# Filler matmuls in the first batch's TensorE gaps, and a filter copy moved ahead of the evacuations

## Chip, cores, metric

One core of a Trainium2 chip (trn2), nothing else running on it. The metric is the device time of one execution in microseconds (us), lowest is best. "Before" and "after" are the kernel before and after the change. PE is TensorE, DVE VectorE, ACT ScalarE, POOL GpSimd. SBUF is the on-chip memory; to evacuate a matmul's result is to copy it from the matmul's output memory into SBUF. A filler is a matmul whose result nobody uses. The clock of PE that a trace calls granted is 1 at full speed and 0.5 at half (in the kernel before, 0.50 stands beside matmuls of 512 columns that start 0.427 us apart, 1.00 in the main stage beside 0.216); fillers are meant to have it released from half to full.

## The reference

A frequency filter along the sequence, then a two-layer MLP with a leaky ReLU, on the same 24064 x 256 tokens:

```python
x: (8, 3008, 256)                      # batch, seq, dim
X = rfft(x, axis=1); Y = X * (filt_r + 1j * filt_i)[None]
y = irfft(Y, n=3008, axis=1).reshape(24064, 256)
h = y @ w_in                           # 256 -> 2048
out = maximum(0.01 * h, h) @ w_out     # 2048 -> 256
```

## The kernel before

The FFT of length 3008 = 94 x 32 is made of matmuls with constants: stage 1 (contraction over the 94 rows, constant `f1`), a transpose on DVE, stage 2 (`fwd2`), the filter product, stage A of the inverse (`inv2`, `inv2x`), another transpose, stage B (constant `i1`). For batches 1 to 7 this is threaded between the MLP's matmuls. For batch 0 there is nothing to thread it into, so it runs by itself at the start; that is the part that the change touches. Line numbers are those of the kernel before.

```python
R1 = 96; N1 = 94                 # f1 has 96 rows, the last two are zero
f1_sb = cpool.tile([R1, N2, P], FP16)          # loaded first, in four slices
x_load(0, ...)                   # x of batch 0: 96 rows, four slices
...
def first_s1(n0, n, kind, copy):               # stage 1, line 250
    ps = bank(kind, n, D)
    for j in range(n):
        nc.tensor.matmul(ps[:, j, :], f1_sb[:N1, n0 + j, :], x_sb[:N1, n0 + j, :],
                         start=True, stop=True)
    spread(big[0], n0, ps, copy)
def first_s2(hf, c, n, on_pool):               # stage 2, line 259, and the filter product
    src = paired(big[1])                       # pairs of fp16, 128 bytes apart
    for j in range(0, n, 4):
        nc.tensor.matmul(ps[...], fwd2, src[:, ds(c + j, 4), ts(hf, DH // 2)], ...)
    # on_pool: ACT copies (line 267), POOL multiplies (270); else DVE multiplies (275)
def first_sa(hf, c):                           # stage A: line 283, ACT evacuates (284)
...
def upper(hf):                                 # line 307: copy the filter to partitions 64-127
    for t, cp in ((fa_sb, act), (fb_sb, dve)):
        cp(t[64:P, :, ts(hf, DH)], t[0:64, :, ts(hf, DH)])
def keep_warm(n):                              # line 312: results unused
    for _ in range(n):
        nc.tensor.matmul(po_ps..., small_sb[:, 0, :], i1_sb[...][:, 0:512], start=True, stop=True)

for g in range(6):  first_s1(4 * g, 4, "ph", (dve, act)[g % 2])
for g in range(4):  first_s1(24 + 2 * g, 2, ...)
t1_part(0, 0), t1_part(0, 1)                   # DVE transposes, line 193
upper(0)
first_s2(0, 8, 8, True); x_load(1); first_s2(0, 0, 8, False)
...                                            # (cut; the order is in the diff below)
keep_warm(5)
for g in range(16): first_sb(g, ...)           # stage B: line 300, copies 303 (two loops, shortened)
...                                            # main loop: MLP, lines 364, 369, 378, 385
```

## Time and profile before

| | before |
|---|---|
| time, first three runs | 788.86, 789.22, 786.11 us |
| span of the profiled run | 787.1 us |
| first slice of x usable (first line 250) | 9.03 us |
| first transposes (line 193) | 18.21 us |
| first line 259 | 20.73 us |
| first line 300 | 41.35 us |
| first MLP matmul (line 364) | 46.75 us |
| end | 740 us after the last row |

Read it as a prologue of 47 us in which a chain passes from engine to engine, and a main part in which PE is full (busy for 725.27 of the 729 us from 58 us on). The stretches, PE timeline and ACT timeline that carry this are shown in the prediction. Three more lines, from the table of fine stretches of the kernel before (stretch, its length, PE busy and count, granted clock, DMA share, GB/s), mark where the clock falls to half and comes back:

```profile
37.00:37.25 0.25, 0.25 (x2) 0.91 0.03 0
37.25:37.50 0.25, 0.25 (x2) 0.50 0.01 0
...
40.50:40.75 0.25, 0.25 (x2) 0.77 1.32 176
```

The first has 0.91 = 0.5 + 0.5 x 0.82, so the fall is 82% into it, at 37.20; in the last, 54% of the stretch is at full clock, so the return is at 40.62.

Two lines of DVE, which is the chain between PE's stages:

```profile
18.21 2.37 DVE L193 STREAM_TRANSPOSE big<-big 128x1024 f32<-128x1024 f32 x2
22.71 1.23 DVE L275 TENSOR_TENSOR fy_h_c<-ph,fa_sb 128x1024 f16<-128x1024 f32 x1 [1.14 <-ACT fx_h_c L267]
```

### The profile page before, as it was taken

The page shows a single profiled execution, that of the slowest core. Times are in us where ns is not written, and L with a number is a line of the kernel's source. Part 1 is how long each engine was busy: PE and PEld are TensorE (multiplying, and loading weights), DVE is VectorE, ACT ScalarE, POOL GpSimd, SP SyncE. Part 2 cuts the span into 40 slices and gives each one's busy share as a digit, 9 for nine tenths or more (in the row PEclk, how much of TensorE's full clock was granted, in tenths as well). Part 3 has the DMA queues.
Part 4 walks back from the last instruction along what each step waited for, and adds up shares of the span by engine and source line. Part 5 has one row for each costly group of instructions (what it writes and reads, how often), then busy time and mean ns, then how long its engine had stood idle before and what let it go on. Part 6 is the DMA issues. An engine that isn't in the chain of part 4 may idle for free.

```text
span 787.1 us, 13542 instructions
## 1 busy us (share of the span) xinstructions
PE 764.4 (97%) x5777; PEld 526.2 (67%) x5777; DVE 366.2 (47%) x457; ACT 556.1 (71%) x790; POOL 148.8 (19%) x122
## 2 busy tenths in 40 slices
PE   3799999999999999999999999999999999999998
PEld 2256677666776667866777667776677666676666
DVE  3858760784317652386415764078432765200000
ACT  3687768776687767877687775967668776666664
POOL 4772400240003400043000510024000340000000
PEclk9999999999999999999999999999999999999999
DMA  9944010501023010511014101050100101101111
GB/s 177 203 62 99 27 41 28 122 28 41 27 67 83 27 41 27 108 41 42 28 41 107 41 28 42 27 119 28 41 28 27 41 27 41 41 28 41 41 41 55
DMA packets 36252, 43.38 MB, mean 55 GB/s; under 512 B 8130, under 2 KB 34370, under 8 KB 35522
## 3 DMA queue, kind: packets, MB, share of 16 engines
q0 software_dynamic: 10000, 16.99, 12.3%
q1 hardware_dynamic: 26192, 25.53, 9.2%
q8 instruction: 45, 0.74, 0.4%
q14 instruction: 15, 0.12, 0.0%
HBM read 34.10 MB, written 24.64 MB: 75 GB/s over the span
## 4 chain that ended last, share of the span: by engine, by line
PE 94%; ACT 2%; DVE 1%; DMA 1%; issue 1%; POOL 0%; ACTq 0%; DVEq 0%; POOLq 0%
PE po_ps L378 41%; PE ph L364 40%; PE pf L170 3%; PE pf L237 2%; PE pf L225 2%; PE pf L210 2%; DMA x_sb<-in_x_dram 1%; PE pf L378 1%; ACT big L181 1%; DVE fy_h_c L275 1%; PE pf L283 1%; ACT gt_c L369 1%; PE ph L250 0%; ACT fa_sb L307 0%; DVE big L193 0%
## 5 line engine op out<-in xcount | busy, mean ns | idle before, releaser
L369 ACT ACTIVATE gt_c<-ph 128x1024 f16<-128x1024 f32 x376 | 384.8, 1024 | 194.8 <-PE ph L364 193.8
L364 PE MATMUL ph<-yt,w_in_sb 128*128 128x512 f16 (+7 forms) x1728 | 386.6, 351 | 0.4 <-ACT yt L303 0.2
L378 PE MATMUL po_ps<-w_out_sb,gt_c 128*128 128x256 f16 x2944 | 381.5, 272 | 0.6 <-ACT ost_c_t L385 0.6
L378 PEld LDWEIGHTS <-gt_c 128*128 128x128 f16 x3008 | 290.7, 98 | 86.7 <-issue 1.7
L364 PEld LDWEIGHTS <-w_in_sb 128*128 128x128 f16 x1728 | 163.0, 98 | 95.2 <-issue 1.0
L218 POOL TENSOR_TENSOR y_b_g<-p_b_g,p_b_g 128x512 f16<-128x512 f32 x84 | 106.9, 1273 | 225.5 <-DVE p_b_g L216 225.5
L193 DVE STREAM_TRANSPOSE big<-big 128x1024 f32<-128x1024 f32 x32 | 55.9, 1847 | 127.0 <-ACT big L181 126.7
L181 ACT CAST big<-pf 128x512 f16<-128x512 f32 x190 | 109.0, 607 | 0.0
L240 DVE CAST yt<-pf 128x376 f16<-128x376 f32 x112 | 56.3, 545 | 85.9 <-PE pf L237 85.9
L214 DVE TENSOR_TENSOR p_b_g<-pf,fa_sb 128x512 f32<-128x512 f32 x84 | 58.1, 692 | 38.5 <-PE pf L210 35.9
L385 ACT COPY ost_c_t<-po_ps 128x256 f32<-128x256 f32 x184 | 69.4, 377 | 6.7 <-PE po_ps L378 5.6
L201 DVE STREAM_TRANSPOSE big<-big 128x1024 f32<-128x1024 f32 x28 | 51.1, 1935 | 34.5 <-ACT big L181 34.5
L215 DVE TENSOR_TENSOR p_b_g<-pf,fb_sb 64x512 f32<-64x512 f32 x84 | 58.2, 693 | 1.1
L216 DVE TENSOR_TENSOR p_b_g<-pf,fb_sb 64x512 f32<-64x512 f32 x84 | 57.4, 684 | 1.1
L132 POOL DMA_DIRECT2D x_sb<-in_x_dram x12 | 6.6, 553 | 256.6 <-PE pf L170 255.8
L237 PEld LDWEIGHTS <-big 128*128 128x128 f16 x448 | 25.7, 98 | 13.2
L170 PE MATMUL pf<-x_sb,f_sb 94*128 94x256 f16 x224 | 33.8, 272 | 0.1
L210 PE MATMUL pf<-big,small_sb 128*128 128x512 f16 x84 | 31.8, 379 | 0.0
L225 PE MATMUL pf<-y_b_g,small_sb 128*128 128x512 f16 x84 | 31.8, 379 | 0.0
L237 PE MATMUL pf<-i_sb,big 128*128 128x94 f16 x448 | 28.7, 206 | 0.0
L170 PEld LDWEIGHTS <-f_sb 94*128 94x128 f16 x224 | 20.9, 97 | 9.5 <-issue 1.3
L250 PE MATMUL ph<-x_sb,f_sb 94*128 94x256 f16 x26 | 6.2, 412 | 10.1 <-DMA x_sb<-in_x_dram 9.6
(45 smaller groups left out, 154.1 us busy)
## 6 DMA issues: line engine op xcount, KB each, us to landing
out_dram<-ost_c_t SPq DMA_DIRECT2D x92, 256.0 KB, 2.1
x_sb<-in_x_dram POOLq DMA_DIRECT2D x6, 1536.0 KB, 11.0
x_sb<-in_x_dram POOLq DMA_DIRECT2D x4, 384.0 KB, 10.2
w_in_sb<-in_moe_w_in_dram POOLq DMA_DIRECT2D x1, 1024.0 KB, 13.0
w_out_sb<-in_moe_w_out_dram POOLq DMA_DIRECT2D x1, 1024.0 KB, 9.8
x_sb<-in_x_dram POOLq DMA_DIRECT2D x1, 1024.0 KB, 8.0
f_sb<-fwd_const SPq DMA_DIRECT2D x4, 192.0 KB, 5.7
fa_sb<-in_filt_r_dram POOLq DMA_DIRECT2D x4, 192.0 KB, 12.3
```

The lines of the kernel that those rows point to most:

```text
L170: nc.tensor.matmul(ps[:, j, :], f1_sb[:N1, n2, :], x_sb[:N1, n2, :], start=True, stop=True)
L181: copy(paired(dst)[:, ds(n0, nn), ds(e0, de)], ps.rearrange("p n (e t) -> p n e t", t=2))
L214: nc.vector.tensor_tensor(p1[:], ps, fa, AL.mult)
L215: nc.vector.tensor_tensor(p2[0:64], ps[64:P], fb[64:P], AL.mult)
L216: nc.vector.tensor_tensor(p2[64:P], ps[0:64], fb[0:64], AL.mult)
L218: nc.gpsimd.tensor_tensor(y1[:], p1[:], p2[:], AL.add)
L237: nc.tensor.matmul(ps[:, j, :], src[:, dt, n2, :], i1_sb[:, n2, :], start=True, stop=True)
L240: copy(yv[:, :, ds(4 * h, 4)], ps.rearrange("p c a -> p a c"))
L364: nc.tensor.matmul(ph[:, j, ds(o, ln)], w_in_sb[:, dt, ts(ct, P)], yts[b % 2][:, dt, ds(lo, ln)], start=(dt == 0), stop=(dt == NDT - 1),)
L369: nc.scalar.activation(gts[ci][:, ds(2 * g, 2), :], ph, AF.Lrelu)
L378: nc.tensor.matmul(po, gts[ci][:, ct, ts(tj, P)], w_out_sb[:, ct, :], start=(ct == 0), stop=(ct == NCT - 1))
L385: nc.scalar.copy(ost[:, tj % 2, :], po)
```

## The change

Intent: keep PE busy in the prologue so that its clock goes to full early and stays there, and let ACT make the second filter copy while it would wait for PE anyway. 53 fillers are added; all fillers read the forward constant `f1`, which lands first, instead of `small` and `i1`.

```diff
     def keep_warm(n):
         for _ in range(n):
-            nc.tensor.matmul(po_ps.rearrange("p a d -> p (a d)"), small_sb[:, 0, :],
-                             i1_sb[:].rearrange("p a d -> p (a d)")[:, 0:512],
-                             start=True, stop=True)
+            nc.tensor.matmul(po_ps.rearrange("p a d -> p (a d)"), f1_sb[:, 0, :],
+                             f1_sb[:, 0:4, :].rearrange("p a d -> p (a d)"), start=True, stop=True)
+    keep_warm(8)
     for g in range(6):
         first_s1(4 * g, 4, "ph", (dve, act)[g % 2])
+        if g % 2:
+            keep_warm(4)
     for g in range(4):
         first_s1(24 + 2 * g, 2, two[g == 3], (act, dve)[g % 2])
+    keep_warm(12)
     t1_part(0, 0, True)(), t1_part(0, 1, True)()
     upper(0)
     first_s2(0, 8, 8, True)
     x_load(1)
     first_s2(0, 0, 8, False)
     t1_part(0, 2, True)()
+    keep_warm(3)
     first_s2(0, 20, 4, True)
+    keep_warm(4)
     first_s2(0, 16, 4, False)
     t1_part(0, 3, True)()
+    upper(1)
     first_sa(0, 0), first_sa(0, 16)
-    upper(1)
+    keep_warm(3)
     first_s2(1, 8, 8, True)
     first_sa(0, 8), first_sa(0, 20)
     first_s2(1, 0, 8, False)
+    keep_warm(3)
     ...
     first_s2(1, 16, 8, False)
+    keep_warm(4)
     first_sa(1, 0)
+    keep_warm(4)
     first_t2(0), first_t2(1)
```

## The prediction

> **What bounds the kernel now.** I read the page first. TensorE (PE) is busy 97% of a 787.1 us span and 94% of the chain that ended last is PE. The busy times by stretch say where the other 3% is:
>
> ```profile
> span 787.1 us, 13542 instructions
> PE 764.4 (97%) x5777; PEld 526.2 (67%) x5777; DVE 366.2 (47%) x457; ACT 556.1 (71%) x790; POOL 148.8 (19%) x122
> ...
> 0.00:47.00 47.00, 28.56 (x202) 13.72 (x203) 28.49 (x29) 25.51 (x38) 31.24 (x31) 0.96 1.08 181
> 47.00:58.00 11.00, 10.62 (x61) 5.79 (x60) 5.75 (x10) 9.93 (x15) 7.46 (x2) 1.00 0.01 2
> 58.00:787.00 729.00, 725.27 (x5516) 506.71 (x5514) 331.95 (x420) 520.68 (x738) 110.09 (x90) 1.00 0.17 48
> ```
>
> The columns after the length are busy PE, weight loads, DVE, ACT, POOL. From 58 us on PE has 3.7 us of gaps in 729: a prologue that ends earlier passes its gain to the end one for one, and nothing after it changes. The change touches only the 47 us of the first batch (the first matmul of line 364 starts at 46.75), where no engine is full. So the question is when that matmul starts afterwards.
>
> The PE timeline of the prologue carries the argument:
>
> ```profile
> 9.03 1.86 PE L250 MATMUL ph<-x_sb,f_sb 94*128 94x256 f16 x8 [9.03 <-DMA x_sb<-in_x_dram]
> 11.46 1.86 PE L250 MATMUL ph<-x_sb,f_sb 94*128 94x256 f16 x8 [0.57 <-DMA x_sb<-in_x_dram]
> 13.79 1.86 PE L250 MATMUL ph<-x_sb,f_sb 94*128 94x256 f16 x8 [0.46 <-DVE big L181]
> 15.51 1.44 PE L250 MATMUL pf<-x_sb,f_sb 94*128 94x256 f16 x6
> ...
> 20.73 1.88 PE L259 MATMUL ph<-big,small_sb 128*128 128x512 f16 x4 [3.36 <-DVE big L193]
> ...
> 25.53 2.74 PE L283 MATMUL pf<-fy_h_c,small_sb 128*128 128x512 f16 x6
> 28.60 1.03 PE L259 MATMUL ph<-big,small_sb 128*128 128x512 f16 x2 [0.33 <-DVE big L193]
> 29.45 1.91 PE L283 MATMUL pf<-fy_h_c,small_sb 128*128 128x512 f16 x6
> 31.20 1.02 PE L259 MATMUL ph<-big,small_sb 128*128 128x512 f16 x2
> ...
> 36.98 2.96 PE L283 MATMUL pf<-fy_h_c,small_sb 128*128 128x512 f16 x7 [0.74 <-DVE fy_h_c L275]
> 39.73 1.69 PE L312 MATMUL po_ps<-i_sb,small_sb 128*128 128x512 f16 x5
> ```
>
> Starts are 0.427 us apart at 512 columns at 25.53 and again at 36.98 (the last of the seven starts at 39.31), where the main stage has 0.216. That is half clock. In fine stretches the granted clock goes to 0.5 at 37.20 and back to 1 at 40.62, and the spacing of line 283 falls to 0.216 at 30.39. The record prints 1.00 from the start although line 250 runs at 0.213 per 256 columns, so I trust spacings there and not the record. So: half clock to 30.39, full to 37.20, half to 40.62.[...]
>
> **One group does not follow the clock.** The line list of line 259 says 588/607/620 ns (min, median, max) for its 12 matmuls, the same at 31.20, when the clock was full, as at 20.73. Line 283 has a minimum of 376. So warming PE buys nothing in line 259.
>
> [...]A window with some 85% of busy stream (26.97 to 30.38) released it here; one as busy with 94-row matmuls (13.31 to 16.73) did not.[...] Line 259 reads 4-byte pairs 128 bytes apart[...].[...]
>
> **The change part by part.**
>
> Filler: 53 new 128x512 matmuls (8 + 3x4 + 12 + 3 + 4 + 3 + 3 + 4 + 4) beside the 5 old ones (keep-warm, line 312), all on the forward constant with 96 rows. At 0.216 us they cost 11.4 us of PE, at half clock 22.6; PE idles over 18 us here. They write the bank that the main stage uses first near 59 us, so they wait for nobody, but a real matmul behind them waits for them.
>
> Stage 1, to the first transposes (18.21 us before). The x slices land at about 9.03, 11.46, 13.7 and 15.5, and no filler moves that. Filler of 8 runs 3.30 to 6.7, cold. Then 8 real to 10.74, 4 fillers cold to 12.45: the second slice waits 1.0 us for them. PE is now without gaps, so it is released[...]. From there: groups 2, 3 end 13.73; filler to 14.6; group 4 waits for DVE's copy of group 2 (13.5 + 1.23), so 14.8 to 15.2; DVE copies it to 16.6; fillers to 16.5; groups 6 to 9 to 17.36; DVE copies groups 7 and 9 (0.69 each) to 18.5. Transposes at 18.55: **0.35 us later**. A release by 10.7 would give 0.6 earlier; at 15.8 it would be 1.5 later. [...]I take 0.4 later. The 12 fillers then end near 20.0, before the transposes (21.0).
>
> From the transposes to 28.5: transposes 2.37, line 259 x4 at its fixed 0.427, DVE products, transpose, products, transpose. DVE is the chain, unchanged. **0**.
>
> 28.54 to 31.8: line 259 x2 (0.85), line 283 x6 at 0.216 (1.3; before four were cold), line 259 x2 (0.85 + 0.17 drain): DVE's products of the second half start at 31.8 instead of 32.31. **0.5 us gained**.
>
> The moved copy: ACT does its 2.75 us filter copy before the evacuations instead of behind them:
>
> ```profile
> 26.60 0.60 ACT L284 CAST big<-pf 128x512 f16<-128x512 f32 x1 [2.47 <-PE pf L283]
> 27.46 0.61 ACT L284 CAST big<-pf 128x512 f16<-128x512 f32 x1 [0.25 <-PE pf L283]
> 28.31 0.60 ACT L284 CAST big<-pf 128x512 f16<-128x512 f32 x1 [0.24 <-PE pf L283]
> 28.94 2.75 ACT L307 COPY fa_sb<-fa_sb 64x3072 f16<-64x3072 f16 x1
> 31.71 1.07 ACT L267 COPY fx_h_c<-ph 128x512 f32<-128x512 f32 x2
> ```
>
> ACT idled 2.47 us up to 26.60, from 24.14. The copy goes there (24.3 to 27.1; the filter's last part lands near 22 to 23 by its issue at 11.61 and 10.4 us to landing), the three evacuations follow to 28.9, and the copies for POOL come at 29.65 instead of 31.71. So POOL's four products end near 34.9 instead of 36.88. This alone moves no end, because DVE's chain ends at 36.93 too; it keeps POOL from becoming the bound when DVE gets earlier. The DVE half of the move changes no DVE order. DVE then ends its four products at 36.45.
>
> 36.45 to the inverse stage: before, 7 matmuls at 0.427 from 36.98, then fillers (two of five warm) to 41.35. After, warm: 7 x 0.216 to 38.0, fillers to 39.15. ACT's four evacuations at 0.54 each from 36.9 end at 39.1 (before 40.58). Line 300 starts at 39.15 to 39.3 instead of 41.35: **2.1 us gained** in all, of which 0.5 is counted above. Its second half needs the last two transposes, at 39.2 + 2.37 = 41.55, when PE gets there at 41.6: just in time. The inverse stage is bound by ACT's copies and keeps its 5.4 us.
>
> Sum: 2.1 gained at line 300, less 0.4 from stage 1: **1.7 us**, so the first line 364 near 45.0. Loads for the main stage are early: the next batch lands before 39 and is used at 46. 788.86 - 1.7 = 787.1 us.
>
> **Rivals.** (1) The filler in stage 1 does not release the clock: 94- and 96-row work may count less, for which the window at 13.31 speaks. Then 20 cold fillers in the in-order PE stream cost 1.71 us per four and 5.1 for the twelve; transposes come 3.8 us late and line 259 later still: a loss of 3 to 4 us, about 792. Against it: [...]the stream is gapless, not 85%. I give it 12%. (2) The clock is released by the first 8 fillers[...] or a little earlier: stage 1 gains 0.6, total 786.1. 20%. (3) Nothing in effect: DVE and DMA set the pace, PE's clock was never on the path. For it: line 259 is deaf to the clock and DVE is the chain from 18 to 37; against it: seven cold matmuls and a cold filler stand openly between 36.98 and 40.6 with ACT waiting 0.24 before each evacuation. It would leave 788.9. 15%.
>
> **Range and chances.** The three runs before spread from 786.1 to 789.2, as much as the effect. Range 784.7 to 789.4. The whole prologue's PE waits cannot give 2% (15.8 us), nor can the fillers cost it, so within 2% is nearly sure.
>
> **What would show it.** Right: line 250 about 0.107 apart per 256 columns after some 13 us; line 259 still near 0.43; line 283 at 0.216 to the end with no half clock after 30; ACT's second filter copy at about 24.5; line 300 starting between 39 and 40.2; first line 364 between 44.5 and 45.5; nothing changed after. Wrong: line 250 cold to the end with transposes after 20 us, or line 283's last seven still cold, or a start of line 364 within 0.5 us of 46.75.

## The result, and the profile after

After: 790.99 us median (790.50 to 791.14, four runs). Before, with one more run: 788.39 (786.11 to 789.22). The ratio is 1.0036, 95% interval 1.0014 to 1.0059. A ratio here is the mean time of one kernel's fast runs over that of the other's of the same rounds, so not quite the ratio of the medians. All runs are fast: none is over 1.5% above the fastest of its kernel. A gain of 1.7 us was predicted; the change costs some 2.6 us by the medians. The call "within 2%" held; the direction and the range did not.

The PE timeline of the kernel after (start, length, engine, line, operation, shapes, count, idle before it):

```profile
3.25 3.59 PE L312 MATMUL po_ps<-f_sb 96*128 96x512 f16 x8 [3.25 <-DMA f_sb<-fwd_const]
7.97 1.86 PE L250 MATMUL ph<-x_sb,f_sb 94*128 94x256 f16 x8 [1.12 <-DMA x_sb<-in_x_dram]
9.63 1.91 PE L312 MATMUL po_ps<-f_sb 96*128 96x512 f16 x4
11.34 1.91 PE L250 MATMUL ph<-x_sb,f_sb 94*128 94x256 f16 x8
...
18.16 1.48 PE L250 MATMUL pf<-x_sb,f_sb 94*128 94x256 f16 x6
19.45 0.63 PE L250 MATMUL ph<-x_sb,f_sb 94*128 94x256 f16 x2
19.87 5.33 PE L312 MATMUL po_ps<-f_sb 96*128 96x512 f16 x12
24.99 1.91 PE L259 MATMUL ph<-big,small_sb 128*128 128x512 f16 x4
26.72 0.83 PE L312 MATMUL po_ps<-f_sb 96*128 96x512 f16 x3
...
33.72 1.47 PE L283 MATMUL pf<-fy_h_c,small_sb 128*128 128x512 f16 x6
...
40.81 1.68 PE L283 MATMUL pf<-fy_h_c,small_sb 128*128 128x512 f16 x7 [0.37 <-DVE fy_h_c L275]
...
48.91 1.29 PE L373 MATMUL ph<-yt,w_in_sb 128*128 128x512 f16 x4 [0.16 <-ACT yt L303]
```

(Line 373 is line 364 of the kernel before, the MLP.) The stream has no gap from 7.97 to 28.8, and yet each eight of line 250 still take some 1.7 us (1.66 to 1.71) from their start to that of what follows, which is 0.213 per 256 columns: half clock, though the trace prints a granted clock of 1.00 there. Twelve fillers take 5.33. Only the three fillers at 26.72 are quick (0.83 = 2 x 0.216 and a modelled end of some 0.39). So the clock was released between 25.0 and 26.7 (the first clock event in the packed trace is at 25.22), and held from there: line 283 has a median of 378 ns in all its 24 matmuls, where it had 613 before. Line 259's matmuls last 589/607/616 ns (min, median, max), as before (588/607/620).

The DVE timeline of the kernel after shows what this did to the chain:

```profile
19.26 0.69 DVE L181 CAST big<-pf 128x512 f16<-128x512 f32 x1 [2.19 <-PE pf L250]
20.11 0.69 DVE L181 CAST big<-ph 128x512 f16<-128x512 f32 x1 [0.16 <-PE ph L250]
20.92 2.37 DVE L193 STREAM_TRANSPOSE big<-big 128x1024 f32<-128x1024 f32 x2
23.32 0.95 DVE L307 COPY fb_sb<-fb_sb 64x3072 f16<-64x3072 f16 x1
26.99 1.22 DVE L275 TENSOR_TENSOR fy_h_c<-ph,fa_sb 128x1024 f16<-128x1024 f32 x1 [2.72 <-ACT fx_h_c L267]
```

DVE waits 2.19 us for PE before three of its five stage-1 copies, the transposes start at 20.92 instead of 18.21 and end at 23.29, and behind its filter copy DVE idles 2.72 us (1.14 before), since the twelve fillers keep PE from line 259 until 24.99.

**The first slice of x lands at a different time in each run** (7.3 to 9.0 us over the traces here), and all of the prologue moves with it. So I compare intervals from the first line 250 of the same trace. The last stretch, from the first MLP matmul to the measured time, is the same 742.2 to 742.5 us in all traces of these kernels (789.03 - 46.75 before, 791.07 - 48.91 after), so the interval to the first MLP matmul is the whole effect.

| trace | to transposes | to line 259 | line 259 to MLP | in all |
|---|---|---|---|---|
| before, profiled run (slow kind, see below) | 9.18 | 11.70 | 26.02 | 37.72 |
| after | 12.95 | 17.02 | 23.92 | 40.94 |

Up to line 259 the change loses 5.3 us, behind it gains 2.1.

### The profile page after: what moved, and what is told of

Read it like the earlier page. It is cut to its first block, busy times and chain, and to the rows that moved or that the text cites. A ratio compares the mean times of both kernels' runs of the same rounds, so it can differ in the third digit from the quotient of the medians.

```text
span 789.2 us, 13649 instructions
## 1 busy us (share of the span) xinstructions
PE 778.6 (99%) x5830; PEld 532.5 (67%) x5830; DVE 366.1 (46%) x457; ACT 555.7 (70%) x790; POOL 149.0 (19%) x122
## 4 chain that ended last, share of the span: by engine, by line
PE 92%; ACT 2%; DVE 1%; issue 1%; ACTq 0%
PE po_ps L387 40%; PE ph L373 40%; PE pf L170 3%; PE pf L237 2%; PE pf L225 2%; PE pf L210 2%; PE pf L387 1%; ACT big L181 1%; ACT gt_c L378 1%; DVE fy_h_c L275 1%; ACT yt L303 0%; PE ph L300 0%; PE pf L283 0%; ACT ost_c_t L394 0%; DVE big L193 0%
## 5 line engine op out<-in xcount | busy, mean ns | idle before, releaser
L312 PE MATMUL po_ps<-f_sb 96*128 96x512 f16 x58 | 21.5, 519 | 3.3 <-DMA f_sb<-fwd_const 3.3
```

## Experiments

Twelve runs were made, two of them of the kernel before itself, in three groups, each beside eleven runs of the kernel before on the group's chip. Correct results in all. Times are medians.

| run | time | ratio to before (95%) | first line 250 to MLP |
|---|---|---|---|
| late_fill | 786.04 | 0.9986 (0.9967 to 1.0004) | 35.86 |
| ones128 | 786.64 | 0.9987 (0.9970 to 1.0004) | 35.34 |
| ones96 | 791.00 | 1.0048 (1.0031 to 1.0064) | 40.94 |
| fill_only | 791.68 | 1.0058 (1.0044 to 1.0073) | 40.81 |
| move_only | 788.05 | 1.0009 (0.9992 to 1.0026) | 37.78 |
| late128 | 787.01 | 0.9996 (0.9980 to 1.0013) | 35.62 |
| rows96 | 786.97 | 0.9996 (0.9981 to 1.0011) | 35.72 |
| no_twelve | 790.80 | 1.0044 (1.0027 to 1.0060) | 39.61 |
| before_again / before_third | 788.74 / 785.48 | one run each | 37.86 / 35.70 |
| probe_rows / probe_two | 899.17 / 1018.63 | one run each, with bursts behind the end | not used |

Theory after the result: a clock that never was released in stage 1 made the fillers cost PE time on the chain. What had to be found is why a gapless stream did not release it: the number of rows (94 and 96 of 128), the data (the constant has zero columns), or the width.

### late_fill: the fillers of stage 1 taken out

```diff
-    keep_warm(8)
-        if g % 2:
-            keep_warm(4)
-    keep_warm(12)
```

> The changed kernel without the fillers of stage 1 (the first 8, the 3 times 4, the 12): only the later fillers and the moved copy stay. Theory: these 32 fillers cost 4.3 us on the path at half clock and release nothing, while all behind them gains 2.1 us. So transposes at 18.2, line 300 near 39.3, first MoE matmul near 44.7, and 2.1 us under the kernel before: ratio to before 0.9973. Rival (the late part gains only because the long early stream released the clock at 25 to 26.7 us): the clock stays at half past 30 us and the gain is under 1 us.

```profile
17.16 2.37 DVE L193 STREAM_TRANSPOSE big<-big 128x1024 f32<-128x1024 f32 x2
19.68 1.88 PE L259 MATMUL ph<-big,small_sb 128*128 128x512 f16 x4 [3.36 <-ACT fa_sb L307]
```

Measured: transposes at 17.16 (9.23 after the first line 250, as before), line 259 at 19.68, MLP at 43.79. The 32 fillers of stage 1 are what costs. The remainder takes 24.11 us from line 259 to the MLP, 1.9 less than the profiled run of before. But the ratio is 0.9986, not 0.9973: half the expected gain, and its interval holds 1. Neither theory said that; before_again and before_third explain it.

### ones128 and ones96: the same fillers on another tile, 128 or 96 rows

The edit, shortened:

```diff
+    warm_sb = cpool.tile([P, 512], FP16, name="warm_sb")
+    nc.vector.memset(warm_sb[:], 1.0)
-            nc.tensor.matmul(po_ps..., f1_sb[:, 0, :], f1_sb[:, 0:4, :]..., start=True, stop=True)
+            nc.tensor.matmul(po_ps..., warm_sb[:128, 0:P], warm_sb[:128, :], start=True, stop=True)  # ones96: [:96]
```

> The changed kernel with its fillers on a 128-row tile of ones (set by DVE at about 1 us) instead of the 96-row forward constant; same number and places. Theory rows: with half of the stream at 128 rows the clock is released in stage 1, by 9 to 15 us; transposes near 18.0 to 19, line 300 near 39 to 40, ratio to before 0.996 to 0.999. Rival data: ones count less than real values and the clock stays at half to 25 us, ratio 1.003 as after the change.

> As the 128-row kernel of ones, but only 96 rows of the tile are used. Theory rows: cold through stage 1 like the changed kernel, transposes near 20.9, ratio to before 1.003. Rival data (zeros in the forward constant are the cause, not rows): released in stage 1 like 128 rows, ratio under 1.

PE timeline of ones128, then of ones96 (line numbers are two higher here: 252 is stage 1, 314 the filler):

```profile
12.71 1.03 PE L314 MATMUL po_ps<-warm_sb 128*128 128x512 f16 x4
13.57 1.04 PE L252 MATMUL ph<-x_sb,f_sb 94*128 94x256 f16 x8
...
16.19 2.75 PE L314 MATMUL po_ps<-warm_sb 128*128 128x512 f16 x12
```

```profile
12.42 1.91 PE L314 MATMUL po_ps<-warm_sb 96*128 96x512 f16 x4
14.13 1.92 PE L252 MATMUL ph<-x_sb,f_sb 94*128 94x256 f16 x8
...
19.25 5.33 PE L314 MATMUL po_ps<-warm_sb 96*128 96x512 f16 x12
```

Same number of instructions, same values, same places; with 128 rows four fillers take 1.03 us, with 96 rows 1.91. The two differ by 4.8 us in their mean time (786.49 and 791.27). So rows made the difference here and the constant's zeros did not: ones96 behaves like the kernel after (40.94 us from the first line 250 to the MLP in both). In ones128 the path was less simple than expected: its first eight fillers, from 1.46 us, released the clock at 5.73, it fell back at 9.14, after PE had waited 3.37 us for x (up to 8.43), and was released again at 12.56 (times of the clock events in its trace). That fall, and not one near 37 us, is what the 0.998 of its profiled run counts. As an explanation of ones96, "96 rows are too few" was the obvious reading. The next probe says it is not quite that.

### probe_rows and probe_two: bursts of one kind of matmul, each from half clock

Behind the end of the kernel before, bursts whose operands POOL rewrites before each (condensed from probe_two; probe_rows has one pass of POOL and 48 matmuls of 512 columns per burst):

```diff
+    for rows, cols, width in (...):
+        for _ in range(3):
+            nc.gpsimd.tensor_scalar(flat[:, 0:3072], wflat[:, 0:3072], 1.0, 0.0, AL.mult, AL.add)
+        for _ in range(28 * 512 // width):
+            nc.tensor.matmul(po[:cols, :width], flat[:rows, 0:cols], flat[:rows, ds(128, width)], ...)
```

> The kernel before with eight bursts of 48 gapless 128x512 matmuls put behind its end. Before each burst GpSimd rewrites the operands (some 8 us or more, in which TensorE is idle and falls back to half clock). Bursts in order: 128 rows of random weights, 96 rows, 112 rows, 128 rows of zeros, 128 rows of ones, 104 rows, 128 rows with 64 stationary columns, 120 rows. Theory rows ([...]94 to 96 of 128 are too few): 128 rows go from 0.427 to 0.216 us spacing[...]; 96 rows stay at 0.427 for all 48 (20.5 us); somewhere between 96 and 128 lies the limit. Rival data (the structural zeros of the forward constant are what counts too little): 96 random rows release like 128; zeros stay at half clock. Rival busy time alone: all eight release[...], and the cold stretch after the change has another cause.

In probe_rows the idle time was only 2.97 us, too short for this purpose: four of the seven bursts that had a gap before them ran at a granted clock of 0.50 at first, the other three at 1.00 throughout. 96 random rows, 112, 120 and 128 rows with 64 columns were released in these, the first within 6.1 us; zeros, ones and 104 rows never were cold, so they said nothing. The released 96 rows contradict my "96 rows stay at half clock". probe_two makes POOL's pass three times, for a longer idle time (8.64 us).

> Bursts behind the kernel before, as in the first probe, but with three GpSimd passes (some 8 us idle) before each, so that every burst starts at half clock. Each is 12 us long at half clock. In order: 128 rows x 512 columns; 96 x 512; 94 x 512; 94 x 256; 96 x 256; 128 x 256; 88 x 512; 64 x 512; 128 rows with 32 stationary columns x 512; 128 x 512 zeros; 128 x 512 ones; 94 x 256 with the forward constant as weights; 4 times (8 of 94 x 256, 4 of 96 x 512), the mix of stage 1. The first probe has shown 96 random rows released[...], so 96 rows alone are enough. Theory rows[...]: 96 x 512 released[...], 94 x 512 and 88 and 64 not at all, the mix not. Theory width (256-column matmuls count less[...]): 94 x 512 released; 94, 96 and perhaps 128 x 256 and the mix not. Theory weights (the constant's zero columns count less): only the burst with the forward constant as weights is not released. Zeros and ones tell whether data counts at all.

PE timeline of probe_two; a burst that stays at half clock takes 12.1 us, one that starts there and is released some 8:

```profile
796.85 8.08 PE L434 MATMUL po_ps<-x_sb 96*128 96x512 f16 x28 [8.64 <-POOL x_sb L439]
813.57 12.13 PE L434 MATMUL po_ps<-x_sb 94*128 94x512 f16 x28 [8.64 <-POOL x_sb L439]
834.34 12.13 PE L434 MATMUL po_ps<-x_sb 94*128 94x256 f16 x56 [8.64 <-POOL x_sb L439]
855.11 8.01 PE L434 MATMUL po_ps<-x_sb 96*128 96x256 f16 x56 [8.64 <-POOL x_sb L439]
871.77 8.21 PE L434 MATMUL po_ps<-x_sb 128*128 128x256 f16 x56 [8.64 <-POOL x_sb L439]
888.62 12.12 PE L434 MATMUL po_ps<-x_sb 88*128 88x512 f16 x28 [8.64 <-POOL x_sb L439]
909.39 12.13 PE L434 MATMUL po_ps<-x_sb 64*128 64x512 f16 x28 [8.64 <-POOL x_sb L439]
930.16 7.99 PE L434 MATMUL po_ps<-x_sb 128*32 128x512 f16 x28 [8.64 <-POOL x_sb L439]
946.78 8.20 PE L434 MATMUL po_ps<-x_sb 128*128 128x512 f16 x28 [8.64 <-POOL x_sb L439]
963.63 8.31 PE L434 MATMUL po_ps<-x_sb 128*128 128x512 f16 x28 [8.64 <-POOL x_sb L439]
980.58 12.11 PE L434 MATMUL po_ps<-x_sb,f_sb 94*128 94x256 f16 x56 [8.64 <-POOL x_sb L439]
1001.33 13.84 PE L434 MATMUL po_ps<-x_sb 94*128 94x256 f16 x48 [8.64 <-POOL x_sb L439]
```

(The bursts at 946.78 and 963.63 are zeros and ones. The last line is the mix, whose two kinds are merged; 13.84 us is all half clock: 32 x 0.213 + 16 x 0.427 + an end of some 0.17. The first burst, 128 rows, followed the main loop without a gap and was never cold.)

The bursts of 96 rows were released (8.08 us at 512 columns, 8.01 at 256), those of 94 rows were not within their 12.13 us at either width, nor those of 88 and 64 rows (12.12 and 12.13). With 128 rows all were released: 256 columns (8.21), 32 stationary columns (7.99), zeros (8.20) and ones (8.31). So in these bursts neither width nor stationary columns nor data decided it, and **the outcome changes between 94 and 96 rows.** The mix of 94 and 96 rows, that of the kernel after, stays at half clock for its 13.84 us, while ones128's mix of 94 and 128 rows was released, at 12.56.

### rows96: the changed kernel with 96 rows in stage 1

Rows 94 and 95 of the constant are zero, and those of x are in SBUF, so they can be multiplied too:

```diff
-            nc.tensor.matmul(ps[:, j, :], f1_sb[:N1, n0 + j, :], x_sb[:N1, n0 + j, :],
+            nc.tensor.matmul(ps[:, j, :], f1_sb[:R1, n0 + j, :], x_sb[:R1, n0 + j, :],
```

> The changed kernel with one edit: the stage-1 matmuls of line 250 take 96 rows instead of 94 (rows 94 and 95 of the constant are zero and those of x are loaded, so the result is the same). The second probe put the limit between 94 and 96 rows. Theory rows: the same gapless stream now counts as enough, the clock is released near 12 to 16 us, line 250 goes from 0.213 to 0.107 us per 256 columns, transposes near 18.5 instead of 20.9, the twelve fillers end before them, line 300 starts some 21 us after the transposes, and the time is 786 to 787.3, ratio to before 0.996 to 1.000, some 4 us under the changed kernel. Rival (something else in stage 1 holds the clock down): no change, ratio 1.003 or more.

PE timeline of rows96:

```profile
8.93 1.87 PE L250 MATMUL ph<-x_sb,f_sb 96*128 96x256 f16 x8 [1.84 <-DMA x_sb<-in_x_dram]
10.59 1.91 PE L312 MATMUL po_ps<-f_sb 96*128 96x512 f16 x4
12.29 1.30 PE L250 MATMUL ph<-x_sb,f_sb 96*128 96x256 f16 x8
13.43 1.03 PE L312 MATMUL po_ps<-f_sb 96*128 96x512 f16 x4
...
17.08 2.75 PE L312 MATMUL po_ps<-f_sb 96*128 96x512 f16 x12
20.76 1.88 PE L259 MATMUL ph<-big,small_sb 128*128 128x512 f16 x4 [0.93 <-DVE big L193]
```

The clock goes to full inside the second eight of line 250 (1.30 us for the eight where 1.86 is cold), near 12.9. The transposes start at 18.24. Two more rows, and the changed kernel loses 4 us of its time (786.87 mean, where the kernel after has 790.90, and ones96 and fill_only 791.3 and 791.6, in other groups; no_twelve, still with 94 rows, has 790.65 in the same group). This settles the cause of the loss. And it is the working that I had predicted, nearly to the digit: transposes expected at 18.55, line 300 at 39.15 to 39.3 (39.25), first MLP near 45.0 (44.65). But it is no faster than before.

### before_again and before_third: why the gain behind stage 1 is worth so little

> The kernel before, to catch the trace of one of its quick runs (clock printed as 1.0, some 786 us), which are about six in ten. Theory: its quick and slow runs differ in whether the clock falls back near 37 us; in a quick one line 283's last seven matmuls are 0.216 apart and line 300 starts near 39.5 to 40 us after the same load time, some 2 us earlier than in the slow one. Rival: they differ in when the first slice of x lands (7.3 to 9.0 us) and not in the clock.

> The same once more, in case the first falls in the other kind.

PE timeline of before_again (788.74 us), then of before_third (785.48 us):

```profile
8.49 1.86 PE L250 MATMUL ph<-x_sb,f_sb 94*128 94x256 f16 x8 [8.49 <-DMA x_sb<-in_x_dram]
...
36.58 3.15 PE L283 MATMUL pf<-fy_h_c,small_sb 128*128 128x512 f16 x7 [0.74 <-DVE fy_h_c L275]
...
46.35 1.28 PE L364 MATMUL ph<-yt,w_in_sb 128*128 128x512 f16 x4 [0.16 <-ACT yt L303]
```

```profile
7.48 1.87 PE L250 MATMUL ph<-x_sb,f_sb 94*128 94x256 f16 x8 [7.48 <-DMA x_sb<-in_x_dram]
...
35.09 1.67 PE L283 MATMUL pf<-fy_h_c,small_sb 128*128 128x512 f16 x7 [0.73 <-DVE fy_h_c L275]
...
43.18 1.28 PE L364 MATMUL ph<-yt,w_in_sb 128*128 128x512 f16 x4 [0.17 <-ACT yt L303]
```

The kernel before has two kinds of run. In one the clock falls to half near 37 us and the last seven matmuls of line 283 take 3.15 us; in the other they take 1.67, and from line 250 to the MLP it is 35.70 us instead of 37.86. The rest of the 3.3 us between the two times is the landing of x (1.0). The kinds can be told by the mean clock: the 3.42 us at half of the profiled run (37.20 to 40.62) in some 787 us make 1 - 0.0022 = 0.998. Of the 33 runs of before beside the experiments, 21 have 0.999 or 1.0 and a mean of 786.43 us (785.45 to 787.32), 12 have under 0.999 and a mean of 788.83 (787.49 to 789.50). (Two of these have 0.996, for which one fall is not enough; no trace of such a run was kept.) The run that was profiled for the prediction was of the slow kind, and so the "2.1 us" were already there in the quick kind. What decides which kind a run becomes is not shown: PE's last waits before the seven matmuls are 0.83, 0.44, 0.33 and 0.74 us in before_again, where the clock fell, and 1.04, 0.22, 0.33 and 0.73 in before_third, where it did not, so nearly the same in sum (2.34 and 2.32).

### fill_only and move_only: the two parts apart

Move_only is the kernel before with `upper(1)` moved; fill_only is after with it moved back.

> All fillers of the change, but the filter copy left behind the evacuations. Theory: the move has no part in the loss; the fillers alone make it. Time within 0.5 us of the changed kernel, ratio to before 1.003 to 1.005. Rival (the move costs, since the evacuations wait for a 2.75 us copy): under 1.002.

> The kernel before with the filter copy moved and no filler. Theory: DVE's chain ends where it did and POOL's earlier end is unused, so within 0.5 us of before, ratio 0.9995 to 1.0005. Rival (the move costs by itself): 1.002 or more.

Fill_only behaves like the kernel after (40.81 against 40.94 us to the MLP), move_only like before (37.78 in a slow-kind trace, against 37.72 and 37.86). Both ratios missed what was expected: 1.0058 where 1.003 to 1.005 was, 1.0009 where 0.9995 to 1.0005 was. Five of move_only's six runs were of the slow kind, which explains its mean; whether the move makes that kind more frequent is not shown. Fill_only's profiled run had x land later than that of the kernel after (9.04 us against 7.97); whether that holds for its other runs was not recorded. Within one kind the move is neutral, as predicted, because DVE's products end with POOL's or after them (36.93 and 36.88 us before, 35.29 and 33.34 in move_only).

### no_twelve: after without the twelve fillers behind stage 1

> The changed kernel without the twelve fillers between stage 1 and the second stage. Theory: at half clock these run from 19.9 to 25.0, the transposes they should cover end at 23.3, so they hold line 259 back 1.6 us; without them 1.6 us less than the changed kernel, ratio to before 1.002 to 1.004. Rival (they release the clock and are needed for the later gain): no better than the changed kernel.

In the trace the interval to the MLP is 39.61 us instead of 40.94, so 1.3 us less, near the 1.6 expected; line 259 follows the transposes. In the time (790.80, ratio 1.0044 where 1.002 to 1.004 was expected) little of this can be seen against the kernel after (790.99); its profiled run had the first slice of x at 9.01 us where the kernel after had it at 7.97. Landing was recorded only in the profiled runs, so how much of the time it took stays open.

### late128: later fillers only, 128 rows of ones

> The later fillers and the moved copy only, with 128-row ones as fillers: the version that should be best. Theory: the clock is released once line 259 starts and never falls back, in every run; so each run at about 786, as the good runs of before, none at 788 to 789.5, ratio to before 0.997 to 0.9995 as before's mean holds some slow runs. Rival (96-row fillers are as good here): the same as the late fillers with the forward constant, 786.0.

All six runs are between 785.67 and 787.58 us with a mean clock of 0.999 or 1.0: no slow kind. The same holds for late_fill (785.69 to 787.36). The spread that remains is as wide as that of x's landing. Their ratios to before, 0.9996 and 0.9986, cannot be told from 1 here. No version beat the quick runs of before; what the later fillers do is that slow runs no longer occur in these twelve.

## Why the prediction was wrong

**The step that failed is in stage 1**: "PE is now without gaps, so it is released". The sums behind it have the clock at full before 13.73, my estimate. The stream had no gaps, and was not released before 25 us. The fillers therefore cost PE time on the chain where they were to save it: transposes 3.77 us later and not 0.35 us (9.18 to 12.95 from the first slice), and line 259 another 1.55 us later behind the twelve (17.02 us from the first slice, 15.47 without them in no_twelve). It was the first rival, to which I gave 12%: "94- and 96-row work may count less". The evidence stood in my own text (a stretch with some 85% of busy stream, 26.97 to 30.38, ended with the clock released, one as busy with 94 rows, 13.31 to 16.73, did not), and I set it aside because the stream was to be gapless, not 85%. probe_two (12.13 us a burst at 94 rows, 8.08 at 96) and rows96 (full clock near 12.9) show that the two rows decided it. A cheap way out was there too: the lines name both row counts, 94 and 96.

**The rival's sizes were right.** Transposes 3.8 us late: 12.95 - 9.18 = 3.77, counted from the first slice. "Line 259 later still": 17.02 - 11.70 = 5.3. A loss of 3 to 4 us: 40.94 - 37.72 = 3.2 against a slow run of before. Its time, about 792, was 1 us too high, and its "20 cold fillers" are 24 between the first slice and line 259.

**"2.1 us gained" behind stage 1** was right for the trace it was worked out from: 26.02 - 23.92 = 2.10. It was the wrong trace to take as typical. Against the quick kind (43.18 - 19.29 = 23.89 us from line 259 to the MLP) the gain is nil, and the loss of the whole prologue is 5.2 us (40.94 - 35.70) and not 3.2. So even a release in time, as in rows96, gives a ratio of 0.9996 and not the 0.9978 that 787.1 over 788.86 is. I had seen that the three runs spread as widely as the effect, and did not ask whether they were two kinds. A reading on the way was off too: in line 283 at 29.45 some two matmuls were cold, not four (0.93 us pass from there to the release at 30.38; the 0.5 us gained still comes out). And the bound under "within 2%" leaves out a step: PE idles 18.4 us of the prologue, over the 15.8, but 9.0 of these pass before the first slice lands.

**Confirmed.** Line 259 does not follow the clock (607 ns median, both kernels). The moved copy alone moves no end (move_only). What comes after the prologue passes one for one. The fall of the clock to half near 37 us does not occur with the later fillers (late_fill, late128, after: line 283's last seven take 1.68 us in each trace).

**The third rival** ("PE's clock was never on the path", 15%) has its result, no gain, behind stage 1 in the quick runs, but not its reason: there the clock is already full when line 283's last seven come (1.67 us). Where it is at half (3.15 us) the MLP starts 2.16 us later, so the clock is on the path.

## What to carry to other kernels

Before filling gaps to raise TensorE's clock, make sure by a trace that what fills them does raise it: between the 94-row matmuls of stage 1, fillers of 128 rows did (four in 1.03 us in ones128), fillers of 96 did not (1.91 in ones96). Check the spacing of matmuls afterwards, because a filler at half clock delayed the real work behind it here: in the kernel after, line 259 started at 24.99, behind twelve such fillers, 1.70 us after the transposes ended (23.29). Where stage 1's matmuls were padded with two zero rows, from 94 to 96, it cost no time (1.87 us for the first eight of line 250 with 96 rows, 1.86 with 94), and the changed kernel's clock went to full near 12.9 instead of 25.2 us. And before working out a gain from one trace, look whether the runs of the kernel fall into groups, and which group the trace is from.
